# One hardware loop in place of an unrolled TensorE program, in a kernel that streams a key-value cache

## The chip, the cores and the metric

The kernel runs on one core of one Trainium2 chip. The metric is device microseconds (us) of one execution. The nine executions of the kernel before agree within about 0.06% (0.5 to 0.7 us of 1,281), so a difference of a microsecond can be told when all runs of one kernel lie below all runs of the other in the same rounds on the same chip.

## The reference, cut to what matters

One decode step of grouped-query attention is mixed with a small dense layer. Two batches, eight key-value heads, 32,768 cached positions of 256 numbers: the two caches are 537 MB in bf16 and each byte is used once.

```python
q = (x @ wq)                                  # 2 batches x 16 heads x 256
scores = einsum("bhqd,bhkd->bhqk", q, k) * Dh ** -0.5
p = softmax(scores)
o = einsum("bhqk,bhkd->bhqd", p, v)
a = o @ wo
out = g * a + (1 - g) * dense(x)              # g, dense: small
```

## The kernel before

A batch and head pair is a *group* (16 of them). A group has two K tiles and two V tiles of 8.39 MB, 64 tiles in all. They pass through a ring of three slots in SBUF; the SyncE queue issues a tile's DMA (a *fill*) when TensorE has released what was in its slot. VectorE transposes a K tile in place, eight instructions a tile; TensorE computes scores from it; a short chain over VectorE, TensorE and ScalarE makes the softmax; TensorE applies the result to V. V runs two tiles behind K.

Each engine's program is written out in full by Python. A first pass counts the events, and a wait is a comparison of a semaphore with a constant:

```python
    def wait(self, stream, key):
        st = self.s.streams[stream]
        ...
        self.eng.wait_ge(st.sem, st.events[key])
```

TensorE's program, with the order of the tiles:

```python
            def S(idx):                       # scores of one K tile: 64 matmuls, 32 weight loads
                ...
                for m in range(NCK // 2):
                    E.wait("dve", ("T", idx, 2 * m + 1))
                    ...
            def PV(v):                        # one V tile: 64 matmuls, 16 weight loads
                if v < LASTV:
                    wait_fill(E, ("V", v))
                ...
            for d in order:                   # K0 K1 K2 V0 K3 V1 K4 V2 ... K31 V29 V30 WO V31
                kind, idx = d
                if kind == "K":
                    S(idx)
                    if idx % NT == NT - 1:
                        g = idx // NT
                        M1(g); M2(g); L(g)    # (three lines) softmax's small matmuls
                elif kind == "V":
                    if idx == LASTV:
                        ...
                    PV(idx)
                    if idx % NT == NT - 1 and idx // NT < GS:
                        OT(idx // NT)
```

The last V tile (V31) arrives in five pieces, after wo, the output weights.

## Time and profile before

| | before |
|---|---|
| time, median of 3 | 1281.15 us (1280.85 to 1281.27) |
| TensorE busy | 733.6 us, 57% |
| VectorE busy | 685.6 us, 54% |
| cache and weight DMA | 547.43 MB, 99.2% of the 16 DMA engines' time |
| TensorE's instruction packets | 29 of 16 KB |

The page of the kernel before: busy time by engine, the DMA row of the 40 slices (9 means 90% or more of the DMA engines' time), the DMA queues (packets, MB, share of 16 engines), and the chain that ended last, by engine.

```profile
PE 733.6 (57%) x4917; PEld 176.3 (14%) x2453; DVE 685.6 (54%) x528; ACT 42.4 (3%) x182; POOL 2.5 (0%) x11
...
DMA  9999999999999999999999999999999999999997
...
q1 hardware_dynamic: 12580, 547.43, 99.2%
q8 instruction: 29, 0.48, 0.2%
q14 instruction: 7, 0.06, 0.0%
...
DMA 58%; DVE 24%; PE 15%; ACT 2%; issue 1%; SPq 1%; another core or an unknown queue 0%; ACTq 0%
```

The DMA engines hardly ever rest (99.2% of their time is taken), so they bound the kernel. Queue 8 carries TensorE's program: 29 packets of 16 KB against 7,454 recorded TensorE instructions, about 257 a packet; 256 instructions are called a block here. A share is an average over the 16 DMA engines, and the run ends with the slowest one (the span ends 5.2 us after the last piece of V31 has landed on its last engine, at 1274.08 us). (In this text the engine that is *last* is always one of these 16 DMA engines.)

The DMA issue view of the kernel before has the fills with the time from issue to landing (median, us):

```profile
ring<-in_A_k_cache_dram SPq DMA_DIRECT2D x32, 46.2
ring<-in_A_v_cache_dram SPq DMA_DIRECT2D x31, 36.6
```

A fill itself takes 19.35 us, so a K fill waits some 27 us and a V fill some 17 us behind other fills. That is the slack of whoever releases the slots. The view of waits shows that TensorE has much idle time as well (engine, line, waited for: us in total, times, longest):

```profile
PE ps_s L399 <- DVE ring L626: 373.8, 63, 19.7
```

One more record is needed here. A fill raises its semaphore once for each of the 16 DMA engines, and the trace has the time of each increment (16 for each fill). The table, worked out from these landing records of the kernel before, gives for some fills when the last engine landed, the gap to the fill before, and how far each of the 16 engines was behind the first, sorted.

```text
landed   gap    us behind the first engine
 369.56  19.35  0.0 0.2 0.4 0.4 0.5 0.5 0.8 0.8 1.5 1.5 1.5 1.5 1.6 1.8 2.0 2.1
 409.78  20.87  0.0 0.2 0.3 0.4 0.5 0.5 0.8 1.5 1.5 1.5 1.5 1.6 1.8 1.8 2.0 3.6
 817.67  20.88  0.0 0.2 0.3 0.4 0.5 0.5 0.8 2.7 3.0 3.0 3.0 3.0 3.1 3.3 3.5 5.1
1224.05  19.34  0.0 0.2 0.3 0.4 0.5 0.8 1.0 3.6 4.4 4.5 4.5 4.5 4.6 4.8 5.0 5.1
1245.01  20.96  0.0 0.2 0.3 0.4 0.5 0.8 1.0 3.7 4.5 4.5 4.5 4.6 4.6 4.9 5.0 6.7
```

All gaps between 40 and 1245 us are 19.34 to 19.37 us except the three above. What a gap has over 19.35 us is called a *late step* here. The engines divide into a group that never falls behind and a group that does so in steps of about 1.5 us: in the last row seven engines are at most 1.0 us behind, one is 3.7 us and eight are 4.5 to 6.7 us behind. Each of the three late steps (1.52, 1.53 and 1.61 us) is in the fill that is under way when a packet of queue 8 comes, and the packets go round eight engines: the engine that is last is hit by packets 8, 16 and 24 (at 398, 804 and 1236 us, counting the first in the profile as 0). The records do not name the engines; an engine was followed from fill to fill by its place in this order.

### The profile page before, as it was taken

Reading aid. Unit: us, or ns where it says so; the run is one execution under the profiler, and the core shown is the slowest. Engines: PE = TensorE matmul, PEld = TensorE weight load, DVE = VectorE, ACT = ScalarE, POOL = GpSimd, SP = SyncE. Lnnn points to the kernel's source line nnn. Section 1 sums busy time; section 2 is a strip of 40 time slices with the busy share of each in tenths; the row PEclk is TensorE's granted clock in tenths of the full one; section 3 lists DMA queues with packets and bytes.
Section 4 is the critical chain, followed back from the end, with each engine's and each line's share of the span. In section 5 each row is a group of like instructions: output and inputs, shape, how many; then the busy total and the mean of one; then the engine's idle time right before and its main releaser. Section 6 shows DMA issues by size and latency. Waiting matters only on the chain.

```text
span 1279.3 us, 8347 instructions
## 1 busy us (share of the span) xinstructions
PE 733.6 (57%) x4917; PEld 176.3 (14%) x2453; DVE 685.6 (54%) x528; ACT 42.4 (3%) x182; POOL 2.5 (0%) x11
## 2 busy tenths in 40 slices
PE   4566566645476454765645666355664546656466
PEld 3111111101011010111101111011110101111024
DVE  1676546745366553556735467453665635566340
ACT  1000000000000000000000000000000000000000
POOL 0000000000000000000000000000000000000000
PEclk9788787867887677887768877778886778876686
DMA  9999999999999999999999999999999999999997
GB/s 409 428 429 443 435 425 434 435 436 429 435 432 431 434 429 439 428 437 434 431 429 433 441 434 425 427 449 433 425 429 437 441 429 425 439 439 430 427 409 301
DMA packets 12772, 547.97 MB, mean 428 GB/s; under 512 B 1336, under 2 KB 3520, under 8 KB 3904
## 3 DMA queue, kind: packets, MB, share of 16 engines
q1 hardware_dynamic: 12580, 547.43, 99.2%
q8 instruction: 29, 0.48, 0.2%
q14 instruction: 7, 0.06, 0.0%
q10 hardware_dynamic: 156, 0.01, 0.0%
HBM read 547.43 MB, written 0.00 MB: 428 GB/s over the span
## 4 chain that ended last, share of the span: by engine, by line
DMA 58%; DVE 24%; PE 15%; ACT 2%; issue 1%; SPq 1%; another core or an unknown queue 0%; ACTq 0%
DMA ring<-in_A_k_cache_dram 56%; DVE ring L626 21%; PE ps_o L272 5%; PE ps_s L399 3%; PE ps_s L272 3%; DMA ring<-in_A_v_cache_dram 2%; PE ps_o L458 2%; DVE mx L630 1%; ACT pexp L555 1%; PE ps_m L422 1%; PE ps_m L417 0%; PE ps_m L412 0%; SPq L315 0%; DVE gmax L632 0%; DVE ls L641 0%
## 5 line engine op out<-in xcount | busy, mean ns | idle before, releaser
L626 DVE STREAM_TRANSPOSE ring<-ring 128x2048 uint32<-128x2048 uint32 x256 | 565.1, 2275 | 318.4 <-DMA ring<-in_A_k_cache_dram 318.4
L399 PE MATMUL ps_s<-ring,Abd 128*128 128x512 bf16 x1024 | 426.1, 416 | 374.2 <-DVE ring L626 373.8
L272 PE MATMUL ps_s<-ring,Abd 128*128 128x512 bf16 x1024 | 422.7, 413 | 0.0
L399 PEld LDWEIGHTS ps_s<-ring,Abd 128*128 128x128 bf16 x1024 | 106.1, 104 | 785.1 <-issue 439.7
L272 PE MATMUL ps_o<-ring,PT 128*24 128x512 bf16 x1440 | 122.8, 456 | 0.0
L646 DVE STREAM_TRANSPOSE PT<-pexp 128x1024 bf16<-128x1024 bf16 x16 | 19.9, 1244 | 82.4 <-PE ps_o L272 82.4
L430 PE MATMUL ps_m<-sel,o_sb 128*128 128x2 f32 x60 | 15.2, 358 | 80.2 <-DVE o_sb L665 80.2
L458 PE MATMUL ps_o<-ring,PT 128*24 128x512 bf16 x480 | 57.0, 465 | 0.0
L665 DVE SCALAR_TENSOR_TENSOR o_sb<-ps_o,mask,o_sb 128x256 f32<-128x256 f32 x105 | 50.8, 484 | 3.7
L630 DVE TENSOR_REDUCE mx<-ps_s 128x1 f32<-128x1024 f32 x16 | 19.6, 1225 | 59.8 <-PE ps_s L272 59.8
L551 ACT ACTIVATE negm<-ps_m 128x1 f32<-128x1 f32 x16 | 2.7, 171 | 1161.2 <-PE ps_m L417 1161.2
L458 PEld LDWEIGHTS ps_o<-ring,PT 128*24 128x24 bf16 x480 | 14.0, 107 | 100.3 <-issue 99.4
L430 PEld LDWEIGHTS ps_m<-sel,o_sb 128*128 128x128 f32 x60 | 13.9, 320 | 99.0 <-DVE o_sb L665 99.0
L422 PE MATMUL ps_m<-ls,ones_f 128*128 128x2 f32 x32 | 8.6, 337 | 28.2 <-DVE ls L641 28.2
L477 PE MATMUL ps_o<-PT,ring 128*128 128x2 bf16 x512 | 14.7, 165 | 9.5 <-DMA ring<-in_A_v_cache_dram 7.7
L641 DVE TENSOR_SCALAR ls<-par,lsum 128x2 f32<-128x2 f32 x16 | 3.7, 229 | 30.7 <-ACT pexp L555 30.7
L546 ACT COPY Abd<-qrep 32x16 bf16<-32x16 bf16 x128 | 19.4, 198 | 0.6
L412 PE MATMUL ps_m<-ident_f,mx 128*1 128x128 f32 x32 | 6.1, 271 | 21.1 <-DVE mx L630 21.1
L555 ACT ACTIVATE pexp<-ps_s,negm 128x1024 bf16<-128x1024 f32 x16 | 17.8, 1115 | 0.5
L673 DVE TENSOR_TENSOR attnT<-ps_o,rl 128x2 bf16<-128x2 f32 x2 | 0.2, 156 | 32.0 <-PE ps_o L477 32.0
L477 PEld LDWEIGHTS ps_o<-PT,ring 128*128 128x128 bf16 x512 | 14.1, 104 | 10.5 <-DMA ring<-in_A_v_cache_dram 8.5
L673 DVE TENSOR_TENSOR attnT<-ps_m,rl 128x2 bf16<-128x2 f32 x30 | 3.4, 158 | 16.6 <-PE ps_m L430 16.6
(63 smaller groups left out, 94.5 us busy)
## 6 DMA issues: line engine op xcount, KB each, us to landing
ring<-in_A_v_cache_dram SPq DMA_DIRECT2D x1, 4096.0 KB, 27.6
ring<-in_A_wo_dram SPq DMA_DIRECT2D x1, 3584.0 KB, 18.3
ring<-in_A_wq_dram SPq DMA_DIRECT2D x1, 3072.0 KB, 10.3
ring<-in_A_v_cache_dram SPq DMA_DIRECT2D x1, 2048.0 KB, 23.2
ring<-in_B_w_dram SPq DMA_DIRECT2D x1, 1568.0 KB, 18.4
ring<-in_B_w_dram SPq DMA_DIRECT2D x1, 1344.0 KB, 13.7
ring<-in_A_v_cache_dram SPq DMA_DIRECT2D x1, 1024.0 KB, 25.1
ring<-in_A_v_cache_dram SPq DMA_DIRECT2D x2, 512.0 KB, 26.1
```

The source lines that it names most:

```text
L272: return e.add_instruction(mybir.InstMatmult(name=f"I-{nc.next_id()}", engine=mybir.EngineType.PE, ldweights=False, ins=[e.lower_ap(x), e. ...
L399: fn = lambda e, o=o, x=x, st=st, sp=sp, s=s, w=w: e.matmul(o, a_win(s, w), x, start=st, stop=sp, skip_group_check=True)
L422: E.ins(lambda e: e.matmul(ps_m[:, C_L:C_L + 2], ones_f[:, :], ls2[:, :], start=True, stop=True), key=("L", g))
L430: E.ins(lambda e, j=j: e.matmul(ps_m[:, C_OT + 2 * j:C_OT + 2 * j + 2], o_sb[:, j:Dh:2], sel[:, :], start=True, stop=True), key=(("OT", g) ...
L458: fn = lambda e, o=o, x=x, wt=wt, st=st, sp=sp, j=j: e.matmul(o, wt, x, start=st, stop=sp, skip_group_check=True)
L477: E.ins(lambda e, kv=kv, r=r, r16=r16, i=i, w=w, j=j, t=t: e.matmul(ps_o[:, 2 * j:2 * j + 2], kv[:, r, j:Dh:2], pt[:, r16, i, 2 * w:2 * w ...
L546: E.ins(lambda e, o=o, Q=Q, c=c: e.copy(o[:, :, c:c + 2], qrep[32 * Q:32 * Q + 32, :, kvh, :, b]), key=(("A", g) if (Q == 3 and c == 16) e ...
L555: E.ins(lambda e: e.activation(pexp[:, :].rearrange("p (r i a) -> p i r a", r=CR, i=2), ps_s[:, :].rearrange("p (i r a) -> p i r a", i=2, ...
L626: E.ins(lambda e: e.transpose(k_words(idx, blk), k_words(idx, blk)), key=("T", idx, blk))
L630: E.ins(lambda e: e.tensor_reduce(mx[:, :], ps_s[:, :], AX.X, ALU.max), key=("MX", g))
L646: E.ins(lambda e: e.transpose(PT[:, :], pexp[:, :]), key=("PT", g))
L665: E.ins(lambda e, p=p, c=c: e.scalar_tensor_tensor(out=o_sb[:, :], in0=p, scalar=mask[:, c:c + 1], in1=o_sb[:, :], op0=ALU.mult, op1=ALU.a ...
```

## The change

The intent: TensorE's program for six K tiles and six V tiles (two is a group, three is the ring, so six is the period of both) becomes a loop body that runs five times. The program is then much shorter. The waits in it compare with a register value, the loop counter times a constant plus a constant. The core of the diff:

```diff
+    def loop(self, n, body, first):
+        self.wait(*first)
...        (first pass: log the waits of each turn; then find v0 and d of each)
+            d = v[2] - v[1]
+            v0 = v[1] - d
+            assert v0 > 0 and d > 0 and all(v[i] == v0 + i * d for i in range(1, n)), reqs
...
+        with self.eng.Fori(0, n) as it:
+            self.at = (it, iter(self.vals))
+            body(0)
...
     def wait(self, stream, key):
...
+        if self.at is not None:
+            nm, v0, d = next(self.at[1])
+            assert nm == stream
+            self.eng.wait_ge(st.sem, self.at[0] * d + v0)
+            return
         self.eng.wait_ge(st.sem, st.events[key])
...
-            for d in order:
...
+            def steps(n):
+                for i in range(UNIT * n, UNIT * n + UNIT):
+                    K(i + LAG)
+                    PV(i)
+                    if i % NT == NT - 1:
+                        OT(i // NT)
+
+            for i in range(LAG):
+                K(i)
+            E.wait("dve", "o0")
+            E.loop((NTILES - LAG) // UNIT, steps, ("dve", ("PT", 0)))
+            PV(LASTV - 1)
...        (FIN, PV(LASTV) and FIN as before)
```

A few `if g >= 1` around waits went away, so that all turns have the same waits, and TensorE now waits once, before the loop, for the first group's softmax (`("PT", 0)`). No other engine's program changed.

More of the change, by code (lines that the diff above doesn't have):

```diff
@@ L31, in __init__ @@
         self.eng = None
+        self.log = None
+        self.at = None
+    def loop(self, n, body, first):
+        self.wait(*first)
+        if self.s.plan:
+            self.logs = []
+            for i in range(n):
+                c0 = self.s.streams[self.name].count
+                self.log = []
+                body(i)
+                self.logs.append((self.log, self.s.streams[self.name].count - c0))
+                self.log = None
+            return
+        st = self.s.streams[self.name]
+        steps = {c for _, c in self.logs}
+        assert len(steps) == 1 and len({len(l) for l, _ in self.logs}) == 1
+        self.vals = []
+        for reqs in zip(*(l for l, _ in self.logs)):
+            nm = reqs[0][0]
+            ev = self.s.streams[nm].events
+            assert all(r[0] == nm for r in reqs)
+            v = [ev.get(key) for _, key in reqs]
+            d = v[2] - v[1]
+            v0 = v[1] - d
+            assert v0 > 0 and d > 0 and all(v[i] == v0 + i * d for i in range(1, n)), reqs
+            assert v[0] in (None, v0) or (nm == first[0] and v0 < v[0] <= ev[first[1]]), reqs
+            self.vals.append((nm, v0, d))
+        with self.eng.Fori(0, n) as it:
+            self.at = (it, iter(self.vals))
+            body(0)
+            assert next(self.at[1], None) is None
+            self.at = None
+        st.count += (n - 1) * steps.pop()
     def ins(self, fn, key=None, stream=None):
@@ L48, in wait @@
         if self.s.plan:
-            self.s.reqs.append((stream, key))
+            if self.log is None:
+                self.s.reqs.append((stream, key))
+            else:
+                self.log.append((stream, key))
+            return
+        if self.at is not None:
+            nm, v0, d = next(self.at[1])
+            assert nm == stream
+            self.eng.wait_ge(st.sem, self.at[0] * d + v0)
             return
@@ L130, in bass_gated_mix__gqa_block_cached__dense_activation_gelu__decode_kernel @@
     LAG = NT
+    UNIT = NB * NT
+    assert (NTILES - LAG) % UNIT == 0
     GS = NG - 1
@@ L409, in M1 @@
                     E.wait("dve", ("RL", g - 1))
-                if g >= 2:
                     E.wait("dve", ("O", g - 2))
@@ L426, in OT @@
                 E.wait("dve", ("OS", g))
-                if g >= 1:
-                    E.wait("dve", ("O", g - 1))
+                E.wait("dve", ("O", g - 1))
                 for j in range(2):
@@ L439, in PV @@
                     E.wait("dve", ("PT", g))
-                    if g >= 1:
-                        E.wait("dve", ("OS", g - 1))
-                    else:
-                        E.wait("dve", "o0")
+                    E.wait("dve", ("OS", g - 1))
                 kv = v_view(v)
@@ L493, in prog_pe, with K @@
             do_FB()
-            for d in order:
-                kind, idx = d
-                if kind == "K":
-                    S(idx)
-                    if idx % NT == NT - 1:
-                        g = idx // NT
-                        M1(g)
-                        M2(g)
-                        L(g)
-                elif kind == "V":
-                    if idx == LASTV:
-                        E.wait_total("d_wo")
-                        E.wait("dve", ("O", NG - 2))
-                        E.wait("dve", "bp")
-                        FIN(0, NCH - 4, "FINA")
-                    PV(idx)
-                    if idx % NT == NT - 1 and idx // NT < GS:
-                        OT(idx // NT)
+            def K(idx):
+                S(idx)
+                if idx % NT == NT - 1:
+                    g = idx // NT
+                    M1(g)
+                    M2(g)
+                    L(g)
+            def steps(n):
[9 more added lines that the diff above has]
+            PV(LASTV - 1)
+            E.wait_total("d_wo")
+            E.wait("dve", ("O", NG - 2))
+            E.wait("dve", "bp")
+            FIN(0, NCH - 4, "FINA")
+            PV(LASTV)
             E.wait("dve", ("O", NG - 1))
```

## The prediction

That the body would stay resident (which means here only that no packet of queue 8 comes in the later turns) was the assumption. The sum is the 1281.15 us of the kernel before less two of three late steps of 1.5 us, 3.0 us: about 1278.2 us. The forecast came to 1278.5 us (1275.5 to 1282.5); among the terms were one for fetches that come back in each turn, and two inside the slack.

> **What bounds the kernel now.** The DMA engines. On the page, the DMA row is 9 in every slice but the last, the main DMA queue's packets fill 99.2% of the 16 engines' time, and 547 MB move at 428 GB/s. The landing records (one per DMA engine and fill) show a metronome: from 40 us to 1224 us one 8.39 MB fill completes every 19.35 us, 433 GB/s. PE is busy 57% and DVE 54%. The chain of waits gives DMA 58%; its DVE and PE pieces run under fills that are already queued. In the DMA issue view K fills land a median 46.2 us after issue and V fills 36.6 us; less the fill's own 19.35 us, TensorE can release a K slot about 17 us late (that issues V), and a V slot about 27 us late (that issues K), before the DMA engines run dry. The tightest release is near the end: wo is issued at 1236.2 us, when the fill ahead lands at 1245.0, so 8.8 us.
>
> **Instruction fetch.** The queue table has TensorE's instruction queue: 29 packets of 16 KB, about one per 256 instructions (7,454 records). Each occupies one DMA engine for about 1.05 us. In the landing records three fills complete 1.5 us late (at 410, 818 and 1245 us), and the spread between the first and last of the 16 engines steps from 2.1 to 3.6, 5.1 and 6.7 us. Those are fetches number 8, 16 and 24: the fetches go round eight engines, and the engine that is last already takes every eighth. So the slowest engine, which ends the run, carries about 4.5 us of fetches in those three steps.
>
> **What the change does.** Five iterations share one body. From the group counts a K tile is 96 TensorE instructions, a V tile 80, a group's softmax and output matmuls about 20: 1,116 per body. Some 66 waits each become perhaps two register operations and a wait, so I estimate 1,250 to 1,400 instructions, five to six blocks of 256.[...] The body should stay resident; fetches fall from 29 to about 13 (12 to 16), and the slowest engine keeps one late step of three: minus 3.0 us.
>
> [...]
>
> **Critical path.** None of the TensorE-side cost; only the fetch packets on the slowest DMA engine.
>
> **Predicted time.** 1278.5 us, 1275.5 to 1282.5. Faster by over 2%: 0.01; within 2%: 0.96; slower by over 2%: 0.03.
>
> **What would show it.** Right: instruction packets near 13; one 1.5 us step instead of three; the fill period still 19.35 us; DMA share still 99%; final landing spread near 3.7 to 4.5 us instead of 6.2; TensorE idle a little longer. Wrong: 29 or more instruction packets, or steps that stay.
>
> **What would make it wrong.** Back edges that refetch the body; register waits costing over 1 us each, which would eat the 17 us of V slack and show as fill gaps over 19.35 us; a slow last group eating the 8.8 us before wo.

## The result, and the profile after

| | before | after |
|---|---|---|
| time, median of 4 | 1281.21 us (1280.85 to 1281.34) | 1279.40 us (1279.20 to 1279.46) |
| ratio, 95% interval | | 0.9986 (0.9969 to 1.0003) |
| TensorE's instruction packets | 29 | 11 |
| last piece of V31 landed | 1274.08 us | 1272.19 us |

In run e2 below, the ratio was 0.9986 again, with an interval of 0.9972 to 0.9999. The first interval includes 1 and the second ends just below it; that the gain is real rests on the runs themselves, as in both the slowest run of the changed kernel (1279.46, 1279.66 us) is over 1 us below the fastest of the kernel before (1280.85, 1280.96 us). The page of the changed kernel, the lines that answer to those of before:

```profile
PE 733.8 (57%) x4917; PEld 176.8 (14%) x2453; DVE 685.6 (54%) x528; ACT 42.4 (3%) x182; POOL 2.5 (0%) x11
...
DMA  9999999999999999999999999999999999999997
...
q1 hardware_dynamic: 12580, 547.43, 99.3%
q8 instruction: 11, 0.18, 0.1%
q14 instruction: 7, 0.06, 0.0%
...
DMA 58%; DVE 23%; PE 16%; ACT 2%; issue 1%; SPq 0%; another core or an unknown queue 0%; ACTq 0%
```

Its DMA issue view and its view of waits:

```profile
ring<-in_A_k_cache_dram SPq DMA_DIRECT2D x32, 45.8
ring<-in_A_v_cache_dram SPq DMA_DIRECT2D x31, 36.6
```

```profile
PE ps_s L446 <- DVE ring L675: 370.1, 63, 18.8
```

TensorE does the same work in the same time and waits as long. The slots are released as before: an even V tile is issued 21.41 us after its K tile has landed (21.42 before, means from the issue and landing records). What changed is queue 8. Its packets come until 287 us, in the first turn (which ends at 310 us), then none until the loop has ended at 1241 us, then four. The landing records of the changed kernel:

```text
landed   gap    us behind the first engine
 369.66  19.35  0.0 0.2 0.3 0.5 0.5 0.8 0.8 1.1 1.1 1.7 1.7 1.9 1.9 2.0 2.1 2.4
 679.28  19.36  0.0 0.1 0.3 0.5 0.5 0.8 0.8 1.1 1.6 1.6 1.9 1.9 1.9 2.0 2.1 2.3
 699.24  19.96  0.0 0.1 0.3 0.5 0.5 0.8 0.8 1.0 1.6 1.6 1.8 1.9 1.9 2.1 2.3 2.9
 951.80  20.34  0.0 0.0 0.3 0.5 0.5 0.7 0.8 1.0 1.5 1.6 1.8 1.8 1.8 2.0 2.3 3.9
1242.20  19.48  0.0 0.0 0.4 0.5 0.5 0.8 1.0 1.3 1.5 1.6 1.8 1.8 1.8 2.0 2.3 4.0
```

The three steps of 1.5 us are gone. Two smaller ones, 0.6 and 1.0 us, are new (and one of 0.13 us). Another engine has become last: one that falls behind by 0.96 us in the fills that land at 408, 699 and 952 us, each of which is under way when an 8 KB packet of queue 14 comes (at 392, 688 and 936 us). Before, that engine was hidden behind the ones that TensorE's packets had delayed (it would be the one that is 3.7 us behind at 1245 us, where those are 4.5 to 6.7 us behind).

Against the 19.35 us period, late steps up to the last whole fill (V30) sum to 4.66 us before and 1.73 us after, 2.9 us less. In the tail 0.9 us is given back: wo lands 10.44 us after V30, where it took 9.54 us before.

### The profile page after: what moved, and what is told of

The parts are those of the page before. It is cut to its first block, busy times and chain, and to the rows that moved or that the text cites. A ratio compares the mean times of both kernels' runs of the same rounds, so it can differ in the third digit from the quotient of the medians.

```text
span 1277.4 us, 8610 instructions
## 1 busy us (share of the span) xinstructions
PE 733.8 (57%) x4917; PEld 176.8 (14%) x2453; DVE 685.6 (54%) x528; ACT 42.4 (3%) x182; POOL 2.5 (0%) x11
## 4 chain that ended last, share of the span: by engine, by line
DMA 58%; DVE 23%; PE 16%; ACT 2%; issue 1%; SPq 0%; another core or an unknown queue 0%; ACTq 0%
DMA ring<-in_A_k_cache_dram 55%; DVE ring L675 20%; PE ps_o L319 5%; PE ps_s L446 4%; PE ps_s L319 4%; DMA ring<-in_A_v_cache_dram 2%; PE ps_o L500 2%; DVE mx L679 1%; ACT pexp L604 1%; PE ps_m L468 1%; PE ps_m L463 0%; PE ps_m L458 0%; DVE gmax L681 0%; DVE ls L690 0%; DVE o_sb L714 0%
## 5 line engine op out<-in xcount | busy, mean ns | idle before, releaser
L675 DVE STREAM_TRANSPOSE ring<-ring 128x2048 uint32<-128x2048 uint32 x256 | 565.1, 2274 | 315.9 <-DMA ring<-in_A_k_cache_dram 315.9
L458 PE MATMUL ps_m<-ident_f,mx 128*1 128x128 f32 x32 | 6.1, 270 | 23.6 <-DVE mx L679 23.6
```

Of the source, the lines that this page charges most:

```text
L675: E.ins(lambda e: e.transpose(k_words(idx, blk), k_words(idx, blk)), key=("T", idx, blk))
```

## The experiments

Eleven runs were made: ten new kernels and the changed one again. Theory A is that each instruction packet delays the one DMA engine that carries it, and that the slowest engine ends the run. The rivals: the gain comes from TensorE's pace (B), a stalled back edge (the branch from the end of the body to its start) costs time (C), what is left at the end is not VectorE's packets (D), a later release of the slots counts (E).

One reading of the landing records bears on B, C and E in all runs at once. The *first* of the 16 engines, which is never behind, ends V30 at 1238.05 to 1238.47 us in the kernel before, the changed one, c1, d1, d2, d3, d4, e1 and e2. A late release would have held it up too; it does so in e3 alone (1240.18 us). The last engine ends V30 anywhere from 1241.3 us (d4) to 1249.4 us (d3), and in every kernel with a full DMA row the profiled span ends 5.2 us after the last piece of V31 has landed. So the differences lie in how far the last engine is behind, V30 and tail together.

### c1: everything but the reuse

The body is written out five times, with the same register arithmetic and register waits, and no branch.

```diff
-        with self.eng.Fori(0, n) as it:
-            self.at = (it, iter(self.vals))
-            body(0)
+        reg = self.eng.alloc_register("turn")
+        self.eng.reg_mov(reg, 0)
+        for k in range(n):
+            self.at = (self.eng.snap(reg, min_val=0, max_val=n - 1), iter(self.vals))
+            body(k)
...
+            self.eng.reg_add(reg, reg, 1)
```

> The whole change except the reuse: the body is written out five times, with the same register arithmetic and the same register-valued waits (some 280 register instructions run, as in the changed kernel), but no branch back. Theory A (the gain is the instruction packets that the slowest DMA engine no longer carries): 29 to 31 instruction packets on TensorE's queue, late steps of 1.5 us as before, time 1280.5 to 1282.5 us, like before. Rival B (the gain comes from TensorE's own program: register waits or another issue timing let it release slots sooner): time about 1279.4 us, like the changed kernel.

Measured: 1281.08 us against 1280.94 us before (ratio 1.0001, 0.9988 to 1.0015). The late steps sum to 4.6 us, as before (4.66); they come as nine of 0.15 to 0.87 us, as three engines take turns at being last, each hit by every eighth packet (5, 13, 21; 8, 16, 24; 9, 17, 25). The DMA queue of c1:

```profile
q8 instruction: 30, 0.49, 0.2%
```

So the register waits neither gain nor cost anything that shows, and the gain of the change is in the reuse of the body.

### c2, c3, c4: padding that was too heavy

Idle semaphore increments were put in front of each tile of TensorE's program: straight (c2), as a small loop (c3), and in the changed kernel (c4).

```diff
# c2 (before) and, with 100 for 64, c4 (after); the same in PV
             def S(idx):
+                for _ in range(64):
+                    E.eng.sem_inc(sch.streams["pad"].sem)
# c3 (before)
+                with E.eng.Fori(0, 16):
+                    for _ in range(4):
+                        E.eng.sem_inc(sch.streams["pad"].sem)
```

> The kernel before, with 64 idle semaphore increments in front of each K tile and each V tile of TensorE's program: 4096 more instructions, 16 more blocks of 256. Theory A: about 45 instruction packets, two more of them on the engine that is last (fetches 32 and 40), so two more late steps of 1.5 us: 1284.2 us (1283.2 to 1285.5). Rival B: TensorE has over 500 us of idle time and 17 us of slack a tile, so a few us a tile cost either nothing or, if the slack is not real, far more than 3 us and in proportion to the increments' own duration; then the looped variant of the same call costs the same.

> The same 4096 increments run by TensorE, but as a small loop of 4 increments that runs 16 times at each place, so TensorE does at least the same extra work while the program grows by only about two blocks. Theory A: about 31 instruction packets and the time of before, 1281.2 us (1280.5 to 1282.8). Rival B: as slow as, or slower than, the straight padding, since it runs 16 branches more at each place.

> The changed kernel with 100 idle increments before each K and each V tile: the loop body is about 2,380 instructions[...]. Theory A: the body no longer stays resident and packets come back in the loop. [...]all of the body is fetched in each turn, about 55 packets, seven on each of the eight engines, 1284 to 1287 us.[...] Rival B (nothing to do with instruction packets): 1279.4 us.

Measured: 1386.97, 1790.06 and 1786.69 us, against 1280.94 us (ratios 1.083, 1.397, 1.396). All three are misses, for one reason that had not been costed: in the trace an increment follows the last after 0.150 us, though its own record is 0.051 us long. 4,096 of them are 616 us, more than the 546 us that TensorE has idle (1279.3 less 733.6). TensorE became the limit. The DMA row and the longest wait of c2, then the wait of c3:

```profile
DMA  9999989989898999979989899997999999799964
...
q8 instruction: 45, 0.74, 0.2%
```

```profile
PE ps_o L464 <- issue: 185.2, 25, 9.4
```

```profile
PE ps_o L466 <- issue: 383.1, 30, 15.4
```

A batch of 64 increments holds TensorE for 9.4 us in c2, and for 15.4 us in c3, where the 16 turns cost 0.96 us each. The times of these runs say nothing about instruction packets. What c2 does show is that the run took in some 510 of the 616 us (616 less the 106 us that it became longer), near the 546 us that the profile calls idle.

c4 still answered one question, by its trace. With a body of 2,383 instructions (9.3 blocks) 12 packets come in each turn, and the four taken back edges are recorded as 6.0 to 6.2 us long; in the changed kernel, with 1,183 instructions, no packet comes and a taken back edge lasts 0.21 to 0.24 us.

```profile
q8 instruction: 65, 1.06, 0.2%
```

### d1: more instructions at hardly any TensorE time

A better way to lengthen the program: cut each 512-column matmul into two of 256 columns under the same loaded weights. The edit for K (that for V is alike):

```diff
-                            if i == 0:
-                                fn = ... e.matmul(o, a_win(s, w), x, ...)
-                            else:
-                                fn = ... keep_matmul(e, o, a_win(s, w), x, ...)
+                            for hv in range(2):
+                                oh, xh = o[:, 8 * hv:8 * hv + 8, :], x[:, 8 * hv:8 * hv + 8, :]
+                                if i == 0 and hv == 0:
+                                    fn = ... e.matmul(oh, a_win(s, w), xh, ...)
+                                else:
+                                    fn = ... keep_matmul(e, oh, a_win(s, w), xh, ...)
```

> The kernel before, with every 512-column matmul of the K tiles and of the V tiles but the last group's cut into two of 256 columns under the same loaded weights: 3,968 more TensorE instructions, 15.5 blocks of 256, with hardly any more TensorE time (a 512-column matmul follows the last after 0.22 us, so its halves should follow after about 0.11 us). Theory A (each instruction packet delays the one DMA engine that carries it by 1.5 us, and the slowest engine sets the end): 44 or 45 packets instead of 29, two more of them on the last engine, 1284.2 us (1283.2 to 1285.5). Rival B (TensorE's own pace decides): TensorE's busy time and its waits for VectorE hardly move, so 1281 us; if TensorE does become slower by tens of us in total, time rises without more late steps of 1.5 us.

Measured: 1283.82 us (1283.75 to 1284.76) against 1281.06 us, 2.76 us more (ratio 1.0023, 1.0010 to 1.0037).

```profile
PE 740.8 (58%) x8885; PEld 176.8 (14%) x2453; DVE 685.9 (53%) x528; ACT 42.4 (3%) x182; POOL 2.5 (0%) x11
...
DMA  9999999999999999999999999999999999999997
...
q8 instruction: 44, 0.72, 0.2%
```

TensorE is 7.2 us busier in all, with its spare time hardly touched, and 15 packets more make the run 2.8 us longer. Theory A said about 3 us, for two packets more (32 and 40) on the engine that is last. The landing records have them: up to V30 there is a late step at packets 8, 16, 24 and 32 (1.2 to 1.3 us each, with 0.3 us more from a second engine), 1.7 us more in all than before; packet 40 comes at 1251 us, during wo, which lands 10.71 us after V30 instead of 9.54 us.

### d2: the same kind of extra instructions inside a resident body

> The changed kernel with the K tiles' matmuls cut in two: 2,048 more instructions run, but the loop body grows only to about 1,570 instructions, which should still stay resident. Theory A: 12 to 14 packets, none between the end of the first turn and the end of the loop, 1279.4 us (1278.6 to 1280.5), as without the split. Rival B (more instructions cost time as such): slower than the changed kernel by about half of what the split costs the kernel before.

The edit is that of d1, for the K tiles alone, in the changed kernel. Measured: 1279.22 us (1279.12 to 1279.31), ratio 0.9986 to the kernel before, just that of the changed kernel. The body has 1,567 instructions (6.1 blocks); no packet comes in the four turns after the first.

```profile
PE 739.0 (58%) x6965; PEld 176.1 (14%) x2453; DVE 685.7 (54%) x528; ACT 42.4 (3%) x182; POOL 2.5 (0%) x11
...
q8 instruction: 13, 0.21, 0.1%
```

2,048 more executed instructions cost nothing that shows where they are not fetched again. With c1 (the gain is not in the register waits) and the first engine's landings, rival B is out.

### d3: a body that is too long

> The changed kernel with all these matmuls cut in two: a body of about 1,950 instructions[...]. The padded body of c4 was fetched anew in each turn (65 packets, 6.1 us at each back edge)[...]. Theory A:[...] the same happens: 45 to 56 packets, four back edges of about 6 us, six to seven packets per engine instead of three to four, 1284 to 1288 us, and the fill period stays 19.35 us but for late steps, so the back-edge stalls cost nothing themselves. If it stays resident: 14 packets and 1279.4 us. Rival C (a back-edge stall of 6 us lies on the critical path): 24 us more, about 1305 us.

"The same" is what c4's trace shows. The edit is that of d1 for K and V, in the changed kernel: the body has 1,951 instructions (7.6 blocks). Measured: 1285.67 us (1285.43 to 1285.75), 4.61 us above before (ratio 1.0036, 1.0022 to 1.0050).

```profile
DMA  9999999999999999999999999999999999999987
...
q8 instruction: 55, 0.90, 0.3%
```

Ten packets come in each turn, and the taken back edges last 6.8 to 8.2 us, 30 us in all. Fills go on through them: the first engine is not held up (V30 at 1238.10 us). The gaps that stand out are six of 1.3 to 1.5 us over the period, in the fills that are under way at packets 8, 16, 24, 32, 40 and 48 (253, 416, 599, 792, 1009 and 1189 us), and after the back edges at 311 and 546 us there is none of these for 55 us or more. A loop can thus be slower than the unrolled program, and the reason is not its stalled branch, which stayed within TensorE's slack here (rival C is out), but the fetches.

### d4, e1, e2: who is last after the change

Two K blocks in one transpose take 128 instructions out of VectorE's program.

```diff
-            return cut(slot_of[("K", idx)], lo, CR * Dh).bitcast(dt.uint32)
+            return cut(slot_of[("K", idx)], lo, 2 * CR * Dh).bitcast(dt.uint32)
...
-                E.ins(lambda e: e.transpose(k_words(idx, blk), k_words(idx, blk)), key=("T", idx, blk))
+                E.ins(lambda e: e.transpose(k_words(idx, blk), k_words(idx, blk)), key=("T", idx, blk + 1))
...
-                    for blk in range(NCK):
+                    for blk in range(0, NCK, 2):
```

> The changed kernel with VectorE's transposes of two K blocks merged into one instruction (128x4096 words instead of twice 128x2048): 128 fewer VectorE instructions, one of its instruction packets of 8 KB fewer, TensorE's program as it is. The landing records of the changed kernel show that one DMA engine is hit by about 0.96 us at 408, 699 and 952 us, just after an 8 KB packet of another engine's program at 392, 688 and 936 us, and that this engine is last from 699 us on. Theory A, with this engine as the new last: one hit fewer, 1278.4 us (1277.6 to 1279.2). Rival D (what is left at the end of the changed kernel is TensorE's own tail or the engine order, not these packets): 1279.4 us.

> The kernel before, with VectorE's merged transposes as in d4. In the kernel before, the engine that is last carries TensorE's packets, not VectorE's. Theory A: one packet of 8 KB fewer, but on an engine that is not last, so no gain: 1281.1 us (1280.7 to 1281.5), where the same edit took 1 us off the changed kernel. Rival D (the merged transposes are simply faster, 557.4 us of VectorE instead of 565.1 us, and that is what d4 gained): about 1 us faster here too, 1280.0 us.

> The changed kernel itself, on the same chip as the two others of this call, so that the three are compared in the same rounds: 1279.3 us (1279.1 to 1279.6), 11 packets of TensorE.

| kernel | time | before in the same rounds | ratio |
|---|---|---|---|
| d4, changed and merged | 1278.33 us (1278.24 to 1278.67) | 1281.06 us | 0.9980 (0.9966 to 0.9993) |
| e1, before and merged | 1281.21 us (1280.79 to 1281.42) | 1281.14 us | 1.0000 (0.9987 to 1.0014) |
| e2, changed, again | 1279.25 us (1279.17 to 1279.66) | 1281.14 us | 0.9986 (0.9972 to 0.9999) |

VectorE's transposes in d4, then in e1 (line, operation, tiles, shapes, count, busy us, mean ns, idle before), and the queue of the other engines' programs in d4:

```profile
L675 DVE STREAM_TRANSPOSE ring<-ring 128x4096 uint32<-128x4096 uint32 x128 | 557.4, 4412 | 320.2 <-DMA ring<-in_A_k_cache_dram 320.2
```

```profile
L626 DVE STREAM_TRANSPOSE ring<-ring 128x4096 uint32<-128x4096 uint32 x128 | 557.5, 4412 | 324.2 <-DMA ring<-in_A_k_cache_dram 324.1
```

```profile
q8 instruction: 11, 0.18, 0.1%
q14 instruction: 6, 0.05, 0.0%
```

The merged transposes take 7.7 and 7.6 us less than the 565.1 us of the kernels without the edit, and this gains nothing in the kernel before. The same edit gains 0.9 us in the changed kernel (1278.33 against 1279.25 us; in d4's own rounds d2, which has the changed kernel's time, took 1279.12 to 1279.31 us, and d4 1278.24 to 1278.67 us), where the engine that carries queue 14's packets is last. In d4 the steps of that engine are at 176, 544 and 874 us, 0.96 to 0.98 us each; in the changed kernel there is one at 99 us beside the three at 408, 699 and 952 us (at 99 us, as its place in the order tells it, while another engine passes it). The steps moved with the length of VectorE's program, and queue 14 has 7, 6 and 5 packets in the changed kernel, d4 and e3 with 528, 400 and 336 VectorE instructions, so most of them are VectorE's (two come at 301 to 309 and at 1077 to 1084 us in every kernel at the full DMA rate, whatever VectorE's count). Rival D is out. d4 is the best version, 2.7 us below before.

### e3: one merge too many

> The changed kernel with four K blocks in one transpose (128x8192 words), 192 VectorE instructions fewer than the changed kernel; TensorE's score matmuls start later, as they wait for four blocks (some 3.6 us more before a K slot is free, out of 17 us). Theory A: at most half a packet more is saved than in d4 and another engine (those that TensorE's body and tail hit) is close behind, so 1277.4 to 1278.5 us, best guess 1277.9. Rival E (the later release counts): slower than d4 by 2 us or more, with gaps between fills over 19.35 us.

The edit is that of d4 with four blocks in one transpose, and TensorE waits for four. (The 3.6 us is an estimate: 16 more score matmuls come after the last transpose, and in the kernel before the 16 from 77.68 to 81.3 us take that long.) Measured: 1280.74 us (1279.52 to 1281.47), 2.4 us above d4. It was run at another time. Its runs scatter by 1.95 us, and the one with a trace is the slowest. Rival E is right here, at one place. The gap between fills is 21.90 us once, at 139.91 us, and 2.55 of the 3.0 us of late steps are there. The SyncE queue in order of time (start, duration) shows the fill that came late, V1, in the kernel before and in e3:

```profile
109.16 0.33 SPq L320 DMA_DIRECT2D ring<-in_A_v_cache_dram  x1
```

```profile
115.77 0.33 SPq L367 DMA_DIRECT2D ring<-in_A_v_cache_dram  x1
```

The fill ahead of it (K3) lands at 115.8 us on its first DMA engine and at 118.0 us on its last, in both kernels. V1, issued 6.6 us later, comes when the first engines have run dry: by the DMA packets' records only 4 to 8 of the 16 engines are busy from 115.5 to 117 us, where the changed kernel has 16. The last engine still had K3 to move when V1 was issued, and why it too fell behind was not followed up. Elsewhere V is issued 24.5 to 29.1 us after its K tile has landed, instead of 21.4 to 22.2 us, and still 9.6 us or more before the fill ahead of it has landed, at no cost that shows.

## Why the prediction was right

The forecast was 1278.5 us and "within 2%"; the time was 1279.4 us, inside the range.

- *The DMA engines bound the kernel.* Right. The 19.35 us period is the same in every kernel but the overloaded c2 to c4.
- *Fetches go round eight engines, and the last one carries 1.5 us for each.* Right. At 1245 us in the kernel before eight of the 16 engines are 4.5 to 6.7 us behind the first, and the last has its steps (1.52, 1.53, 1.61 us) in the fills of packets 8, 16 and 24. d1 and d3 add packets and time (15 packets, 2.8 us; 26 packets, 4.6 us), d2 adds 2,048 instructions with only two packets more than the changed kernel, and no time. c1 shows the round of eight on three engines.
- *The body stays resident.* Right, by queue 8: no packet came in four further turns of bodies of 4.6 blocks (the changed kernel) and 6.1 blocks (d2), and 10 and 12 packets came in each turn of bodies of 7.6 blocks (d3) and 9.3 blocks (c4). Where between 6.1 and 7.6 blocks a body becomes too long, and why, was not shown.
- *29 packets to about 13 (12 to 16).* A little high: 11, just under the range. The register arithmetic is about one instruction a wait, not two (59 recorded in each turn, against the forecast's some 66 waits); the body has 1,183 instructions, not 1,250 to 1,400.
- *"the slowest engine keeps one late step of three: minus 3.0 us."* This is the term that was mis-sized, in two ways. None of TensorE's steps was left on that engine up to 1242 us. But the run does not end with *that* engine: the forecast had no place for the next one, the engine that carries VectorE's packets, which is 4.0 us behind the first at the last whole fill. Late steps fell by 2.9 us, and 0.9 us of it went again in the tail, so that the last landing came 1.9 us earlier and the time fell by 1.8 us. That the late steps fell by about the 3.0 us forecast, and that the final spread of 4.45 us lies within the forecast's 3.7 to 4.5 us, is luck: one step of TensorE's was expected to be left, and what is left (1.73 us) belongs to another engine and another program. A packet of queue 14 comes at 1245 us, during wo, and the last engine's lag grows there from 4.0 to 4.6 us; that this packet is the whole 0.9 us was not tested.
- *None of the TensorE-side cost is on the path.* Right. TensorE's first small matmul waits 23.6 us in total for VectorE in the changed kernel and 21.1 us before, in 16 groups, so the register waits lengthen the softmax chain by about 0.16 us a group there. c1 says that this costs nothing that shows.
- *17 us of slack for V, and the tightest release before wo.* Right in the steady state, incomplete at the start: V1 is issued only 8.8 us before the fill ahead has landed on its last engine, and 6.7 us before it has on its first. The change does not touch this; e3 ran into it. wo, which the forecast took for the tightest, is issued 2.1 us before the first engine has ended V30; in d3 it is issued 5.0 us after that, and still lands 9.50 us after V30 on the last engine, so there the last engine decides.
- *"Back edges that refetch the body", as what would make it wrong.* They did not with this body of 4.6 blocks: a taken back edge was recorded as 0.21 to 0.24 us, the one that was not taken as 0.08 us. With bodies that were too long they did (6.0 to 6.2 us in c4, 6.8 to 8.2 us in d3), and in d3 the slack held them: the first engine ends V30 at 1238.10 us.

Why a packet of 16 KB delays its engine by 1.5 us stays open. Its own record is 0.96 to 1.11 us long in the kernel before, and a 64 KB packet of a fill is recorded as 2.42 us, so that 16 KB at that rate would be 0.6 us.

## What to carry to other kernels

In a kernel whose DMA engines hardly ever rest (99.2% here), ask which of the 16 engines ends last and what only that engine carries: a queue with 0.1% of the bytes (0.48 of 548 MB) decided this change, because each of its packets that could be followed put 1.2 to 1.6 us on one engine. The loop gained 1.8 us here with bodies that stayed resident (4.6 and 6.1 blocks of 256 instructions) and lost 4.6 us with one that did not (7.6 blocks), and it gained until the next engine was last; look for that one before sizing the gain. And cost an idle filler instruction from a trace (0.150 us each here) before using it as a neutral one.
